# Thresholded attention and a quick-GELU MLP on one core: three of five threshold subtractions of the first eight head pairs on GpSimd, two-server transfers in the planner, new ranks

## The chip, the cores and the metric

The kernel runs on one core of a Trainium2 chip. The metric is device time in microseconds (us) of that core for one launch; lower is better. The time before the change is the median of three runs. One more execution was recorded by the profiler. Engines are named as the profile names them: PE (TensorE), DVE (VectorE), ACT (ScalarE), POOL (GpSimd), SP (SyncE, which here only issues transfers).

## The reference

Attention in fp32 with 8 batches, 8 heads, 576 rows and head size 64. Scores below the row maximum minus `tau` are dropped, the rest goes through a softmax. The result, laid out as 4608 tokens by 512, goes through an MLP with 2048 hidden units.

```python
scores = scale * np.matmul(q, k.transpose(0, 1, 3, 2))
thresh = np.max(scores, axis=-1, keepdims=True) - tau
scores = np.where(scores >= thresh, scores, -1000000000.0)
scores = scores - np.max(scores, axis=-1, keepdims=True)
attn = np.exp(scores)
attn = attn / (np.sum(attn, axis=-1, keepdims=True) + 1e-09)
x = np.matmul(attn, v)            # then (B,H,S,D) -> (B*S, H*D)
h = x @ w_in
g = h * (1.0 / (1.0 + np.exp(-1.702 * h)))
out = g @ w_out
```

The two weight matrices arrive as 64-bit floats, so the kernel turns them into fp32 itself.

## The kernel before, in words

**Attention.** Two heads make a pair; there are 32 pairs (`NP`), four to a batch, numbered from 0. A pair's transposed scores are cut into nine key blocks of 64, kept two by two in tiles of 128x1152 fp32: four full tiles and a tail tile of 128x576. For a pair the steps are, with their functions:

- `load_qk`, `load_v`: transfers issued by SP; `prep` (L477): two 32x32-block transposes on DVE.
- `scores_run` / `scores` (L493): matmuls on PE in 64x64 tiles; `keep` (L510): ACT copies each block from PSUM to SBUF.
- `in_groups` with max (L516): DVE transposes and reduces each tile; `over_tiles` (L525) and `over_halves` (L536, L542): DVE ends the row maxima and takes tau off.
- The row of thresholds is spread over all partitions: `turn_rows` (L553) on DVE, then `row_out` to DRAM and `row_in` back by SP. Pair 2 uses `spread_max` on DVE instead (`BY_DMA`).
- `sub` (L580): DVE subtracts the thresholds from each of the five tiles, in place. Both operands and the result are in SBUF.
- `mask` (L586) and `exps` (L590): ACT zeroes out what lies below and takes the exponential.
- `values` (L601) and, for pairs 0 to 4, `sums_by_pe` (L601): PE. From pair 5 on the softmax sums are made by DVE: `in_groups` with add, `over_tiles`, then either `one_group` (L643, L647) with `spread_sums` (L684, L686), used for pairs 5 to 7, or from pair 8 on `turn_sums` (L658 to L663) with the transfers `sums_out` and `sums_in` (`SUMS_BY_DMA`).
- `place_x` (L703): DVE multiplies by the reciprocal sums into the MLP's input tile.

**Weights.** 32 pieces of 128x512 numbers (16 of `w_in`, 16 of `w_out`). For each, `load_w` issues two transfers from POOL's queue (L428, L429); DVE and ACT make fp32 of it: `cv_ex` (L439, DVE), `cv_power` (L447, ACT), `cv_frac` (L453 and L457, DVE), `cv_end` (L465, DVE). `hold` (L484) is a small POOL copy that keeps the loads behind the preps of pairs 2 and 3.

**MLP.** 18 blocks of 256 tokens. The first two go together (`mm1_0` L758, `gelu_0` L764, `mm2` L740), and start when pairs 0 to 3 are placed and the first pieces of `w_in` are ready; blocks 2 to 13 use `mm1` (L718), `gelu` (L730) and a seven-product scheme for the second matrix (`product` L909, sums `s_sums` L875 to L877 and `s_last` L888 on POOL); the last four use it for both matrices.

**Order.** No engine's order is left to a compiler. Each piece of work is a `task` with an engine, a cost in us, a rank and what it needs; `run_in_order` plays the costs through and, whenever an engine is free in that play, gives it the ready task of lowest rank. The kernel is emitted in the order that results, so a rank or a cost changes only the order of instructions on each engine. At run time every engine works through its list in order and waits on semaphores. Ranks are the pair's number plus a bias by kind of task, in tables `EARLY` (pairs 0 to 3), `SECOND` (4 to 7), `LATER` (8 to 31), `CV` for conversions and `W_RANK`. MLP matmuls have the last rank, so PE takes them when no attention work is ready. A DMA is one SP task with a fixed `lag` until the data counts as there.

Of the kernel before, what the change touches and what calls it, by code (L numbers as in the profile page):

```python
# [19 lines left out]
P = 128  # L20
# [10 lines left out]
def kernel(  # L31
# [84 lines left out]
    stop = const.tile([P, 1], FP32, name="stop")  # L116
    shift = const.tile([P, 1], FP32, name="shift")
# [9 lines left out]
    for x in ("raw0", "raw1", "qkT0", "qkT1", "mb"):  # L127
# [6 lines left out]
        "exps": -11.47,  # L134
        "in_groups": 5.75,
        "keep": 10.66,
        "load_qk": -0.27,
        "load_v": 4.86,
        "mask": -2.66,
        "one_group": -15.86,  # L140
        "one_row": 12.67,
        "over_halves": -7.01,
        "over_tiles": -4.01,
        "place_x": -17.11,
        "prep": -11.73,
        "row_in": 20.49,
        "row_out": 4.47,
        "scores_run": 12.45,
        "spread_max": -1.73,
        "spread_sums": 7.14,  # L150
        "sub": 9.27,
        "sums_by_pe": 0.27,
        "sums_in": -9.39,
        "sums_out": 2.13,
        "turn_rows": -12.55,
        "turn_sums": -0.41,
        "values": 14.64,
        "w_sum": 4.11,
        "x_sum": -14.1,
    }  # L160
    SECOND = {
        "exps": -7.29,
        "in_groups": 20.95,
        "keep": 16.67,
        "load_qk": -8.88,
        "load_v": 5.53,
        "mask": 2.36,
        "one_group": 2.55,
        "one_row": -2.71,
        "over_halves": -12.07,  # L170
        "over_tiles": 2.86,
        "place_x": -20.26,
        "prep": 3.49,
        "row_in": -19.42,
        "row_out": -24.08,
        "scores_run": -7.99,
        "spread_max": -3.11,
        "spread_sums": -2.29,
        "sub": 14.98,
        "sums_by_pe": 35.93,  # L180
        "sums_in": 7.43,
        "sums_out": 4.05,
        "turn_rows": -3.84,
        "turn_sums": 4.03,
        "values": 11.79,
        "w_sum": -10.45,
        "x_sum": -10.98,
    }
    LATER = {
        "exps": 2.01,  # L190
        "in_groups": 10.37,
        "keep": -0.02,
        "load_qk": -6.6,
        "load_v": 3.77,
        "mask": 14.79,
        "one_group": 4.78,
        "one_row": -14.98,
        "over_halves": 1.09,
        "over_tiles": -6.27,
        "place_x": -0.34,  # L200
        "prep": 2.34,
        "row_in": 4.02,
        "row_out": 2.64,
        "scores_run": -11.25,
        "spread_max": -9.44,
        "spread_sums": -6.73,
        "sub": 2.14,
        "sums_by_pe": 1.46,
        "sums_in": 3.78,
        "sums_out": 2.16,  # L210
        "turn_rows": 12.26,
        "turn_sums": 0.29,
        "values": -10.38,
        "w_sum": 6.61,
        "x_sum": 6.02,
    }
    CV = {
        "cv_end": -8.05,
        "cv_ex": 2.22,
        "cv_frac": -11.72,  # L220
        "cv_power": -4.72,
        "load_w": -7.79,
    }

    LAG = {"PE": 0.26, "DVE": 0.18, "ACT": 0.22, "POOL": 0.18}

    QUARTERS = ("scores", "scores_run", "values", "sums_by_pe")
# [12 lines left out]
    FIRST, LAST = -9.0, 1000.0  # L240
    need, follows = {}, {}

    def run_in_order():
# [12 lines left out]
        while events:  # L256
# [18 lines left out]
            for engine, queue in ready.items():  # L275
                if engine in busy:
                    continue
                for rank, i in sorted(queue):
                    if engine == "PE" and held_for not in (None, i):
                        continue  # L280
                    take = tasks[i][6]
                    least = need.get(i, {})
                    if all(free[pool] >= take.count(pool) for pool in set(take)) and all(
                        free[pool] >= least[pool] for pool in least
                    ):
                        break
                else:
                    continue
                queue.remove((rank, i))
                for pool in take:  # L290
                    free[pool] -= 1
                busy.add(engine)
                cost = tasks[i][1]
                if engine == "PE":
                    held_for = follows.get(i)
                    last, mode = mode, tasks[i][3].__name__ in QUARTERS
                    cost += ENTER[mode] if mode != last else 0.0
                heapq.heappush(events, (now + cost, 0, i))
                started += 1
                tasks[i][3](*tasks[i][4])  # L300
# [3 lines left out]
    JOINT = 7  # L304

# [183 lines left out]
    def scores(n, j):  # L489
# [8 lines left out]
        if j == NK - 1:  # L498
            del mats[n, 0], mats[n, 1]
# [32 lines left out]
    def over_halves(n):  # L532
        r = stats[n, ALU.max]
        o = work.tile([P, QB], FP32, name="fold", tag="fold", bufs=1)
        for x in (1, 3) if n in BY_DMA else range(4):
# [3 lines left out]
            )  # L539
        if n in BY_DMA:  # L540
# [10 lines left out]
    def turn_rows(n):  # L551

        nc.vector.transpose(out=flat[1], in_=flat[0])  # L553

# [23 lines left out]
    def sub(n, t):  # L578
        s = sT[n, t].rearrange("p u h s -> p u (h s)")
        nc.vector.tensor_tensor(  # L580
            out=s, in0=s, in1=mbs[n].unsqueeze(1).to_broadcast(list(s.shape)), op=ALU.subtract
        )
# [24 lines left out]
    def values(n, tiles):  # L607
# [4 lines left out]
        if n < NPAIR:  # L612
# [334 lines left out]
    nc.gpsimd.memset(ones, 1.0)  # L947
    nc.gpsimd.dma_start(
# [26 lines left out]
    BY_PE = 5  # L975
    BY_DMA = (0, 1, *range(3, NP))
    SUMS_BY_DMA = range(8, NP)
    LEAD = 6
    WHOLE = 6

    FFU = 1.727
    T_RANK = FIRST

    W_RANK = (0, 12.87, 12.51, 22.24, 0, 4.97)
    ready_w, w_loads, w64 = [], [], 0
    for i in range(len(pieces)):
# [10 lines left out]
        a = task("POOL", 1.1, rank, load_w, i, after=w_loads[-1:], take=place, lag=9.0)  # L997
        w_loads.append(a)
        e = task("DVE", 0.345, rank, cv_ex, i, after=[a])
        m = task("ACT", 0.67, rank, cv_power, i, after=[e])  # L1000
        a = task("DVE", 1.1, rank, cv_frac, i, after=[e])

        over = [ready_w[y] for y in range(i) if i >= n_in and stage(y) == (i - n_in) // PER_STAGE]
        ready_w.append(task("DVE", 0.61, rank, cv_end, i, after=[a, m] + over, give=place))
# [191 lines left out]
    for n in range(NP):  # L1196
# [5 lines left out]
        slow = 1.1 if n < NPAIR else 1.0  # L1202
# [3 lines left out]
        cost = 3.5 if NPAIR <= n < 2 * NPAIR else 2.0  # L1206
        lag = (4.6, 3.0)[n] if n < 2 else 10.0 if n < 2 * NPAIR else 3.0
        lq = task("SP", cost, r - 2.0, load_qk, n, 0, q0, after=behind, take=own(n, "raw0"), lag=lag)
        lk = task(
            "SP", cost if n else 0.1, r - 2.0, load_qk, n, 1, q1, after=behind,  # L1210
            take=own(n, "raw1"), lag=lag,
        )
        v_m = f"v_m{n % 2}"
        lv = task("SP", 2.4, r + (1.85 if n < 2 else -1.2), load_v, n, after=lvs[-1:], take=(v_m,), lag=3.0)
        lvs.append(lv)
        pq = task("DVE", 0.69, r, prep, n, 0, after=[lq], take=own(n, "qkT0"), give=own(n, "raw0"))
# [45 lines left out]
        else:  # L1262
            for js in [range(x, x + 3) for x in range(0, NK, 3)] if n >= WHOLE else [[x] for x in range(NK)]:
# [4 lines left out]
                    give=own(n, "qkT0", "qkT1") if js[-1] == NK - 1 else (),  # L1268
# [4 lines left out]
        a = task("DVE", 0.35, r, over_tiles, n, ALU.max, after=mx)  # L1273
        a = task(
            "DVE", 0.8 if n in BY_DMA else 1.05, r, over_halves, n, after=[a, tau_done],
            take=("row",) if n in BY_DMA else (),
        )
        if n in BY_DMA:
            a = task("DVE", 0.21, r, turn_rows, n, after=[a])
            a = task("SP", 0.6, r, row_out, n, after=[a], lag=3.3)  # L1280
            m = task(
                "SP", 1.0, r, row_in, n, after=[a], take=own(n, "mb"), give=("row",),
                lag=5.2,
            )
        else:
            m = task("DVE", 0.78, r, spread_max, n, after=[a], take=own(n, "mb"))
        spread[n] = m
        ws, subs = [], [m]
        for t in range(NKT + 1):
            tail = t == NKT  # L1290
            a = task(
                "DVE", 0.67 if tail else 1.35, r, sub, n, t, after=subs[-1:],
                give=own(n, "mb") if tail else (),
            )
            subs.append(a)
# [5 lines left out]
        if n < NPAIR:  # L1301

            pv = den = None
            for t in every:
                first = t == 0
                den = task(
                    "PE", (0.97 if t < NKT else 0.484) * slow, r, sums_by_pe, n, [t], True, after=[ws[t], den],
                    take=("psM", "psM") if first else (),
                )
                pv = task(  # L1310
                    "PE", (0.97 if t < NKT else 0.484) * slow, r, values, n, [t], after=[ws[t], den, pv, lv],
                    take=("psA",) if first else (), give=(back[t],) if t < NKT else ("s_t", v_m),
                )
            su = []
            a = task("DVE", 1.07, r, one_row, n, after=[den], give=("psM", "psM"))
        else:
# [3 lines left out]
            if n < BY_PE:  # L1320
                a = task("PE", 4.36, r, sums_by_pe, n, every, False, after=ws + [pv], take=("psA",), give=back)
                a = task("DVE", 1.07, r, one_row, n, after=[a], give=("psA",))
            else:
                su = [
                    task("DVE", 0.66 if t == NKT else 1.27, r, in_groups, n, t, ALU.add, after=[ws[t]])
                    for t in range(NKT + 1)
                ]
                a = task("DVE", 0.35, r, over_tiles, n, ALU.add, after=su + [pv], give=back)
                if n in SUMS_BY_DMA:
                    a = task("DVE", 1.35, r, turn_sums, n, after=[a], take=("row_s",))  # L1330
                    a = task("SP", 0.6, r, sums_out, n, after=[a], lag=3.3)
                    summed[n] = task("SP", 1.0, r, sums_in, n, after=[a], take=("rc",), give=("row_s",), lag=5.2)
                else:
                    a = task("DVE", 1.6, r, one_group, n, after=[a])
# [41 lines left out]
```

## Time and profile before

| | us |
|---|---|
| median of three runs (1318.22 to 1318.92) | 1318.74 |
| the profiled execution, its own time | 1317.94 |
| its span, first to last instruction | 1316.2 |
| PE busy in the span | 1260.9 |
| DVE busy | 1006.1 |
| ACT busy | 646.6 |
| POOL busy | 249.0 |
| PE busy in 0 to 120 us | 79.00 |
| PE busy in 120 to 200 us | 79.05 |
| PE busy in 200 to 300 us | 94.19 |
| PE busy in 300 to 700 us | 397.42 |
| PE busy in 700 to 1100 us | 398.52 |
| PE busy in 1100 to 1316 us | 212.76 |

The profile is of one execution. A row of groups gives the line, the engine, the operation, what is written and read with shapes, how often, then busy time, mean duration in ns, and the idle time of the engine before these instructions with what ended it. The table's windows are read against their length: 120 us with 79.00 busy leave 41.0 idle. A clock below 1.00 is the share of full speed that TensorE was granted.

### The profile page before, as it was taken

How to read it: one execution, taken by the hardware profiler on the slowest of the kernel's cores; microseconds unless marked ns; L12 is line 12 of the kernel's file. 1: busy time of each engine (PE TensorE's matmuls, PEld its weight loads, DVE VectorE, ACT ScalarE, POOL GpSimd, SP SyncE). 2: the span in 40 equal slices, each digit the busy share in tenths (PEclk: the TensorE clock that was granted, in tenths of full speed). 3: DMA queues.
4: the chain of work that ended last, by engine and by line, in shares of the span. 5: the costliest groups of instructions: out<-in, count | busy, mean ns of one | idle time of the engine just before them, and what ended most of it. 6: DMA issues, size and time to landing. Idle time of an engine off the chain costs nothing. (4 is left out here: it accounts for less than half of the span.)

```text
span 1316.2 us, 22807 instructions
## 1 busy us (share of the span) xinstructions
PE 1260.9 (96%) x9128; PEld 975.6 (74%) x9128; DVE 1006.1 (76%) x1610; ACT 646.6 (49%) x830; POOL 249.0 (19%) x291
## 2 busy tenths in 40 slices
PE   5669999999999999999999999999999999999998
PEld 2346864457887777777778888777777778888887
DVE  7989999898888887788777877777888863652642
ACT  4876666576554555555554555454556540210210
POOL 1201211012031211213021303030212117120120
PEclk8879999999999999999999999999999999999999
DMA  8976766545323223212213222323122110000000
GB/s 152 293 189 207 230 207 149 112 77 100 85 55 71 55 55 71 51 50 54 58 42 72 55 71 55 71 55 71 36 55 54 36 46 8 9 1 25 8 0 32
DMA packets 258819, 102.88 MB, mean 78 GB/s; under 512 B 233754, under 2 KB 243994, under 8 KB 258714
## 3 DMA queue, kind: packets, MB, share of 16 engines
q1 hardware_dynamic: 244986, 63.40, 22.4%
q0 software_dynamic: 11360, 37.74, 9.3%
q8 instruction: 71, 1.16, 0.4%
q10 hardware_dynamic: 2368, 0.30, 0.2%
q14 instruction: 34, 0.28, 0.1%
HBM read 87.51 MB, written 9.69 MB: 74 GB/s over the span
## 5 line engine op out<-in xcount | busy, mean ns | idle before, releaser
L516 DVE TRANSPOSE_TENSOR_REDUCE part<-arena 128x36 f32<-128x1152 f32 (+1 forms) x295 | 357.5, 1235 | 41.9 <-ACT arena L510 32.4
L718 PE MATMUL hps<-xT,w_in 128*128 128x256 f32 x1536 | 337.2, 380 | 0.5 <-DVE arena L730 0.4
L718 PEld LDWEIGHTS hps<-xT,w_in 128*128 128x128 f32 x1536 | 290.7, 190 | 45.9 <-issue 5.7
L586 ACT ACTIVATE arena<-arena 128x1152 f32<-128x1152 f32 (+1 forms) x160 | 169.4, 1059 | 144.0 <-DVE arena L580 143.8
L510 ACT COPY arena<-ps 128x576 f32<-128x576 f32 x288 | 170.7, 647 | 115.3 <-PE ps L493 111.9
L580 DVE TENSOR_TENSOR arena<-arena 128x1152 f32<-128x1152 f32 (+1 forms) x158 | 201.1, 1313 | 20.5 <-DMA arena<-row 20.5
L909 PE MATMUL ops<-w_out,arena 128*128 128x256 f32 x896 | 202.4, 380 | 1.8 <-DVE arena L730 1.8
L590 ACT ACTIVATE arena<-arena,shift,scl 128x1152 f32<-128x1152 f32 (+1 forms) x160 | 200.3, 1252 | 4.1
L493 PE MATMUL ps<-arena 64*64 64x288 f32 x2304 | 174.7, 420 | 22.9 <-DVE arena L477 15.3
L909 PEld LDWEIGHTS ops<-w_out,arena 128*128 128x128 f32 x896 | 169.3, 190 | 28.7 <-DVE arena L730 3.1
L875 POOL TENSOR_TENSOR arena<-arena 128x256 f32<-128x256 f32 x56 | 49.7, 888 | 647.1 <-DVE arena L730 543.9
L601 PE MATMUL pv<-arena 64*64 64x288 f32 x2176 | 159.7, 408 | 0.0
L727 ACT ACTIVATE th<-hps 128x512 f32<-128x512 f32 x112 | 66.0, 589 | 186.0 <-PE hps L718 171.8
L909 PE MATMUL ops<-arena 128*128 128x256 f32 x672 | 150.7, 380 | 0.7 <-DVE osb L931 0.7
L493 PEld LDWEIGHTS ps<-arena 64*64 64x64 f32 x2304 | 84.0, 137 | 90.8 <-ACT arena L510 30.4
L909 PEld LDWEIGHTS ops<-arena 128*128 128x128 f32 x672 | 127.1, 190 | 20.4 <-issue 2.2
L601 PEld LDWEIGHTS pv<-arena 64*64 64x64 f32 x2176 | 82.1, 134 | 54.1 <-issue 10.0
L931 DVE SCALAR_TENSOR_TENSOR osb<-ops,osb 128x256 f32<-128x256 f32 x98 | 39.3, 413 | 97.9 <-PE ops L909 90.6
L730 DVE SCALAR_TENSOR_TENSOR arena<-th,hps 128x512 f32<-128x512 f32 x96 | 64.2, 669 | 46.7 <-ACT th L727 46.4
L740 PE MATMUL ops<-w_out,arena 128*128 128x512 f32 x128 | 57.2, 600 | 3.2 <-DVE w_out L465 2.2
L758 PE MATMUL hps<-xT,w_in 128*128 128x256 f32 x256 | 56.4, 381 | 0.0
L888 POOL TENSOR_TENSOR arena<-arena 128x512 f32<-128x512 f32 x28 | 35.6, 1272 | 108.3 <-PE ops L909 108.3
(115 smaller groups left out, 1044.7 us busy)
## 6 DMA issues: line engine op xcount, KB each, us to landing
arena<-in_v_dram SPq DMA_DIRECT2D x128, 144.0 KB
arena<-in_q_dram SPq DMA_DIRECT2D x128, 72.0 KB
out_dram<-osb SPq DMA_DIRECT2D x36, 256.0 KB
arena<-in_k_dram SPq DMA_DIRECT2D x124, 72.0 KB
arena<-row SPq DMA_DIRECT2D x62, 144.0 KB
arena<-row_s SPq DMA_DIRECT2D x48, 144.0 KB
w_out<-in_moe_w_in_dram POOLq DMA_DIRECT2D x12, 512.0 KB, 9.5
arena<-in_moe_w_out_dram POOLq DMA_DIRECT2D x12, 512.0 KB, 6.3
```

The costliest lines, as they stand in the source:

```text
L493: nc.tensor.matmul(ps[ts(c, KT), h, 0:SH], lhsT=mats[n, 1][ts(h, D), ts(j, KT)], rhs=mats[n, 0][ts(h, D), ts(c, SH)], start=True, stop=True,)
L510: nc.scalar.copy(out=sT[n, t][:, u], in_=pss.pop((n, j))[:, :, 0:SH])
L516: nc.vector.tensor_reduce(out=stats[n, op][:, t * 2 * QB : min(2 * t + 2, NK) * QB], in_=sT[n, t].rearrange("p u h (g d) -> p (u h g) d", ...
L580: nc.vector.tensor_tensor(out=s, in0=s, in1=mbs[n].unsqueeze(1).to_broadcast(list(s.shape)), op=ALU.subtract)
L586: nc.scalar.activation(out=s, in_=s, func=AF.Prelu, alpha=STEEP)
L590: nc.scalar.activation(out=s, in_=s, func=AF.Exp, scale=scl, bias=shift)
L601: nc.tensor.matmul(o[c][ts(h, D), 0:SH], lhsT=left(j, h)[ts(c, KT)], rhs=sT[n, t][ts(c, KT), u, h, :], start=(j == 0), stop=(j == NK - 1),)
L718: nc.tensor.matmul(hidden[j][:, ts(f, BLK)], lhsT=w_in[:, c, ds((f * HF + j) * P, P)], rhs=xTs[blk][:, c, :], start=(c == 0), stop=(c == N ...
L727: nc.scalar.activation(out=ths[j], in_=hidden[j], func=AF.Tanh, scale=GELU_SCALE / 2)
L730: nc.vector.scalar_tensor_tensor(out=g[:, :, j, :], in0=two(ths.pop(j)), scalar=1.0, in1=two(hidden.pop(j)), op0=ALU.add, op1=ALU.mult,)
L740: nc.tensor.matmul(acc[i], lhsT=g0[:, j, ts(i, P)], rhs=w_out[:, j, :], start=(j == 0), stop=(j == NFC - 1),)
L909: nc.tensor.matmul(banks[blk][k][:, ts(o, HM)], lhsT=left[:, j, :], rhs=right[:, j, :], start=(j == 0), stop=(j == HF - 1),)
```

## The change

- Subtraction: `sub` runs on GpSimd for tiles 1, 3 and 4 (the tail) of pairs 0 to 7, and stays on VectorE for tiles 0 and 2. Its waits within a pair are per engine.
- Sums: pairs 5, 6 and 7 go by `turn_sums` and two transfers each way, as pairs from 8 on did.
- Planner: a transfer is now a task of its own on one of two servers, "DMS" for what SP issues and "DMW" for the weights, taken first come first served; SP tasks keep only their issue cost. Costs of conversions and some others are new; `cv_frac` and `cv_end` are charged `SHARED` = 0.2 us more.
- Ranks: all four tables and `W_RANK` are new.
- A second way to apply thresholds by PE (`row_blocks`, `again`, `mask_one`) is added but its set of pairs, `TWICE`, is empty. Its two constant tiles are still filled at the start, on POOL ahead of the transfer of tau.

```diff
+    minus = const.tile([P, 2, KT], FP32, name="minus")
+    own_row = const.tile([P, QB // 2], FP32, name="own_row")
...
     EARLY = {
...
-        "in_groups": 5.75,
+        "in_groups": 13.97,
...
-        "sub": 9.27,
+        "sub": 6.54,
...
     CV = {
-        "cv_end": -8.05,
-        "cv_ex": 2.22,
-        "cv_frac": -11.72,
-        "cv_power": -4.72,
-        "load_w": -7.79,
+        "cv_end": -15.81,
+        "cv_ex": -1.62,
+        "cv_frac": -18.99,
+        "cv_power": -9.27,
+        "load_w": -20.76,
     }
...
+    def transfer(by, time, a, give=(), lag=1.7):
+        return task(by, time, FIRST, moved, after=[a], give=give, lag=lag)
...
+    TWICE = ()
+    BY_POOL = dict.fromkeys(range(8), (1, 3, 4))
...
     def sub(n, t):
         s = sT[n, t].rearrange("p u h s -> p u (h s)")
-        nc.vector.tensor_tensor(
+        engine = nc.gpsimd if t in BY_POOL.get(n, ()) else nc.vector
+        engine.tensor_tensor(
             out=s, in0=s, in1=mbs[n].unsqueeze(1).to_broadcast(list(s.shape)), op=ALU.subtract
         )
...
+    nc.gpsimd.memset(minus, 0.0)
+    nc.gpsimd.memset(own_row, 0.0)
+    for x in range(4):
+        nc.gpsimd.memset(minus[ts(x, 32), x % 2, :], -1.0)
+        nc.gpsimd.affine_select(
+            out=own_row[ts(x, 32)], in_=own_row[ts(x, 32)], compare_op=ALU.not_equal, fill=1.0,
+            base=-(QB // 2) * (x // 2), pattern=[[-1, QB // 2]], channel_multiplier=1,
+        )
...
-    SUMS_BY_DMA = range(8, NP)
+    SUMS_BY_DMA = range(5, NP)
...
+    SHARED = 0.2 if BY_POOL else 0.0
...
-    W_RANK = (0, 12.87, 12.51, 22.24, 0, 4.97)
+    W_RANK = (22.52, 3.88, 13.03, 23.19, 4.19, 0.55)
...
-        a = task("DVE", 1.1, rank, cv_frac, i, after=[e])
+        a = task("DVE", 1.14 + SHARED, rank, cv_frac, i, after=[e])
...
-        ready_w.append(task("DVE", 0.61, rank, cv_end, i, after=[a, m] + over, give=place))
+        ready_w.append(task("DVE", 0.7 + SHARED, rank, cv_end, i, after=[a, m] + over, give=place))
...
-        ws, subs = [], [m]
+        spread.setdefault(n, m)
+        ws, subs = [], [(m, None)]
...
+            pool = t in BY_POOL.get(n, ())
             a = task(
-                "DVE", 0.67 if tail else 1.35, r, sub, n, t, after=subs[-1:],
+                "POOL" if pool else "DVE", (1.45 if pool else 0.67) if tail else 2.7 if pool else 1.35,
+                r, sub, n, t, after=[y for y, x in subs if tail or x in (None, pool)],
                 give=own(n, "mb") if tail else (),
             )
-            subs.append(a)
+            subs.append((a, pool))
```

## The prediction, as put on record

> **What bounds the kernel now.** I read the page's busy table first, then busy time by stages.
>
> ```profile
> PE 1260.9 (96%) x9128; PEld 975.6 (74%) x9128; DVE 1006.1 (76%) x1610; ACT 646.6 (49%) x830; POOL 249.0 (19%) x291
> ```
>
> PE is busy in 1260.9 of 1316.2 us, so 55.3 us are all that any reordering can win. The windows say where they lie (columns: length, PE, weight loads, DVE, ACT, POOL, PE clock, DMA share, GB/s).
>
> ```profile
> 0.00:120.00 120.00, 79.00 (x1016) 45.33 (x1016) 103.53 (x179) 87.16 (x110) 18.74 (x43) 0.87 0.81 208
> 120.00:200.00 80.00, 79.05 (x494) 59.24 (x490) 77.93 (x135) 45.16 (x58) 15.93 (x29) 1.00 0.67 214
> 200.00:300.00 100.00, 94.19 (x727) 49.38 (x727) 92.04 (x142) 68.01 (x86) 10.11 (x11) 0.98 0.57 116
> ```
>
> 41.0 of the 55.3 us are idle before 120 us, 6.8 between 120 and 300, 7.5 in the remaining thousand. DVE is busy in 103.5 of the first 120 us (it can't start before 6.8) and in 77.9 of the next 80. PE's waits in 0 to 120 us name their releasers:
>
> ```profile
> PE ps L493 <- DVE arena L477: 15.3, 3, 8.3
> PE den L601 <- DVE r L632: 12.9, 2, 10.8
> PE den L601 <- DVE w_out L457: 7.0, 1, 7.0
> PE den L601 <- ACT arena L590: 2.8, 6, 1.1
> ```
>
> The first three add up to 35.2 of 41.0 us. So up to about 240 us DVE's list sets the pace; afterwards PE does. The MLP's first matmul starts at 117.6 us. A microsecond taken off DVE's list ahead of that brings the rest of PE's work forward by about one, as long as DVE also keeps up from 120 to 240, where it is as full.
>
> **What the Trainium skill says.** "GPSIMD Engine Reference", section 3.1 Elementwise — side-by-side cycle accounting, puts a two-input operation on GpSimd at about 2.6 cycles of 1.2 GHz per element, roughly twice VectorE. The trace agrees: POOL's undisturbed two-input operations took 0.73 us at 256 elements and 1.27 at 512, so 2.11 ns an element. "SBUF — State Buffer", section Who interferes with whom, says that GpSimd shares one pair of SBUF ports with VectorE, exclusively for a whole instruction, and that a VectorE instruction with two SBUF inputs is held by a GpSimd one that reads SBUF. The trace shows it, in DVE's and POOL's order of time (start, duration):
>
> ```profile
> 1088.52 0.69 DVE L797 TENSOR_TENSOR arena<-w_in 128x512 f32<-128x512 f32 x1
> ...
> 1092.53 1.75 DVE L806 TENSOR_TENSOR xT<-xT 128x512 f32<-128x512 f32 x1
> ```
> ```profile
> 1092.02 1.71 POOL L797 TENSOR_TENSOR arena<-w_in 128x512 f32<-128x512 f32 x1
> ```
>
> 0.69 us is the undisturbed length of that shape. POOL's instruction waited some 0.44 us (1.71 for 1.27), then ran to 1093.73; DVE's, begun at 1092.53, took 1.06 us too long. "VectorE: DVE Perf Modes", section Mode 2×_2P — use both read ports for one tensor, says that one-source fp32 operations from SBUF may take both ports too. The two L536 instructions at 291.2 us took 1.14 instead of 0.49 beside POOL, which agrees; a conversion beside a POOL operation isn't in this trace.
>
> **The change part by part.** I sum against the profiled execution's 1317.94 us (span 1316.2 and 1.7 around it); the median of the runs is 0.8 above it. Durations, from DVE's groups up to 280 us:
>
> ```profile
> L580 DVE TENSOR_TENSOR arena<-arena 128x1152 f32<-128x1152 f32 x36 | 47.0, 1342 | 7.5 <-DMA arena<-row 7.5
> L457 DVE SCALAR_TENSOR_TENSOR w_out<-w_out 128x512 int32<-128x512 int32 x16 | 11.1, 695 | 0.5
> L439 DVE TENSOR_SCALAR arena<-arena 128x512 uint32<-128x512 uint32 x16 | 6.8, 426 | 0.0
> L580 DVE TENSOR_TENSOR arena<-arena 128x576 f32<-128x576 f32 x7 | 5.2, 749 | 0.0
> ```
>
> *Subtractions off DVE.* 8 pairs x (2 x 1.342 + 0.749) = 27.5 us, half before 117.6 us.
>
> *Sums of pairs 5 to 7.* `one_group` with `spread_sums` took 0.73 + 0.70 + 0.27 + 0.78 = 2.48 us on DVE; `turn_sums` of pair 8 took 0.71 + 0.18 + 0.27 + 0.21 = 1.37. Three times the difference is 3.3 us. Six transfers out and six in are added. For pair 8 SP began them at 289.48, DVE placed its result at 299.61: the way by DRAM is some 8 us longer in latency than DVE's own 1.05. Pair 7 is placed at 276.40 and block 2 starts on PE at 280.23. Its sum can begin before its values do (261.6), so I take nothing; without that lead up to 4 us. Gross saving: 30.8 us.
>
> *Subtractions on POOL.* 1.27 + 640 x 2.11 ns = 2.62 us for a full tile and 1.41 for the tail: 16 x 2.62 + 8 x 1.41 = 53.2 us. As POOL idled most of the first 240 us, its own time is hidden. Three of them take 6.65 us against the 6.12 of five on DVE before, so ACT, which needs all five, gets its last tile at about the same time. Behind a POOL subtraction that waits for its row stand `hold`, `load_w` and their two transfers a piece. POOL waited 36.3 us for a free stage at one point, so I take nothing; if its refills get late, up to 4 us.
>
> *Collisions.* This is the unknown. While POOL holds the ports, DVE goes on through `in_groups` (L516), preps and what reads PSUM, and stops at the first instruction with two SBUF inputs or two ports: the remaining subtractions, conversions, `over_halves`. Nearest rows: 32 conversions x (0.42 + 0.42 + 0.70 + 0.69) = 71.4 us, remaining subtractions 16 x 1.342 = 21.5, `over_halves` about 8; 101 us of some 190 after the removal, about half. Upper bound: every hold stops DVE for its whole length, 53.2 us. Lower bound: the change's own charge, 0.2 on two tasks of 32 pieces, 12.8 us. A gain is excluded, as a lock only delays. If half of the holds met such an instruction at once, it would be 27; as a burst of L516 (1.35 us each) hides part, I take 22.
>
> *Start.* Ten small POOL instructions now stand before the transfer of tau. Fills of 128x32 and 128x64 took 0.12 and 0.15 us, so some 1.5 us in all; tau's transfer was issued at 1.39, took 3.9, and DVE read it at 9.16. There is 3.1 us of cover: 0. An `affine_select` isn't in the trace; if it is ten times a fill, 4 us of start are lost.
>
> *Ranks and servers.* They remove no instruction. What they could win is DVE's own idle time after its start, 12.5 us from 10 to 240, its longest waits 3.7 for a row behind loads on SP (SP issued q and k of a later pair ahead of `row_out` at 82.19). What they could lose is as much, since the new order was laid out with subtractions on DVE at 1.35, that is without collisions. Value 0, from -5 to +8. `LATER` acts where PE idles 7.5 us in 1016; at most a few of these either way.
>
> *Sum.* 30.8 - 22 = 8.8 us less DVE work up to 240 us. ACT (87.2 us of the first 120) and DMA (share 0.81) are late next, but have that much room. 1317.94 - 8.8 = 1309.1; with the 0.8 to the median, 1310.
>
> **Rivals.** *Slower: DVE behind POOL's locks.* POOL's tile 1 and DVE's tile 0 are released by the same row. Whoever comes second waits, and then DVE's tile 2 finds POOL in tile 1: 2.4 us a pair. If in the two holds that follow (tile 3 and tail, 4.0 us) conversions stand next, 60% of them are lost as well: 4.8 a pair, 38.5 in all. Then DVE has 7.7 us more to go through, and the time is 1317.94 + 7.7 + 0.8 = 1326. For it: subtractions and conversions were back to back from 34.7 to 64 us, and the new `CV` ranks put conversions ahead of both `in_groups` and `sub`. Against: `in_groups` is the largest group and passes. It decides from 30.8 us of collisions on, 58% of POOL's hold time.
>
> *The saving is parked.* PE's start may be set by ACT, the loads (DMA share over 1.00 in three of the first eight slices of 10 us) or the row trips, and DVE only gets idle: 1318.7, within 0.2%. Against: DVE's waits for a row were only 3.9 us up to 240.
>
> *Collisions at their lower bound.* 30.8 - 12.8 = 18.0 saved: 1317.94 - 18.0 + 0.8 = 1301. For it: PE idles 41 us, enough to be won. Against: the alternation near 1090 us.
>
> **Numbers.** Forecast 0.40 at 1310, its own range 1305 to 1315; collisions at the lower bound 0.11 at 1301; parked 0.11; slower 0.38 at 1326. About 0.2% (2.6 us) is what a measurement of this kernel can tell from no change. Faster 0.51, same 0.11, slower 0.38. The range reaches from 1299, a little past the small-collision case, to 1331, the slower rival with the late tau or the refills on top; beyond each lies about one in ten.
>
> **What would show it.** Right: POOL has 24 more two-input instructions of 2.6 and 1.4 us or longer, DVE's busy sum to 300 us changes little, since waits for the port count as duration, L457, L465 and L580 get longer means, and the MLP's first matmul comes some 5 us before 117.6. Means of L580 above 2.0 us or of L457 and L465 above 1.0 would show the slower rival; PE waiting for a row or for L510 the parked one. What would make it wrong in another way: stalls after 300 us from the new `LATER` ranks, or block 2 waiting for pair 7.

## The result and the profile after

The changed kernel took 1352.17 us in the median of four runs (1350.22 to 1353.76), the kernel before 1318.83 beside it: ratio 1.0247, 95% interval 1.0224 to 1.027. The forecast was 1310 and the end of its range 1331. The loss of 33.3 us is more than four times the 7.3 us that the slower rival had (1326 against 1318.7). The profiled execution took 1350.22 us, with a span of 1348.4.

The busy table of the page after:

```profile
PE 1267.5 (94%) x9128; PEld 984.7 (73%) x9128; DVE 1014.9 (75%) x1577; ACT 638.1 (47%) x830; POOL 312.5 (23%) x325
```

DVE has 33 instructions fewer and is busy 8.8 us longer; POOL is busy 63.5 us longer. PE has the same matmuls and 6.6 us more busy time (its granted clock in the first 120 us is 0.80 instead of 0.87). Its idle time went from 55.3 to 1348.4 - 1267.5 = 80.9 us. The stages, in the same columns as before:

```profile
0.00:120.00 120.00, 64.33 (x801) 38.92 (x805) 100.45 (x134) 74.36 (x94) 52.41 (x63) 0.80 0.75 191
120.00:200.00 80.00, 73.61 (x586) 58.46 (x579) 70.18 (x120) 37.89 (x50) 18.78 (x25) 0.93 0.62 180
200.00:300.00 100.00, 87.69 (x564) 45.41 (x566) 83.10 (x123) 61.73 (x78) 34.47 (x23) 0.95 0.57 134
```

PE idles 55.7 us before 120, 6.4 up to 200 and 12.3 up to 300: 74.4 against 47.8, so all the idle time that was added lies ahead of 300 us. In the first 120 us DVE is as busy as before (100.45 against 103.53) and gets through 134 instructions instead of 179; 12 of the 45 that are missing are subtractions that went to POOL. The MLP's first matmul comes at 134.8 us instead of 117.6. DVE's groups up to 300 us answer to those shown of before (L633 is the old L580, L469 the old L457, L451 the old L439, L477 the old L465; the number after the busy time: mean ns):

```profile
L633 DVE TENSOR_TENSOR arena<-arena 128x1152 f32<-128x1152 f32 x16 | 40.2, 2537 | 10.9 <-DMA arena<-row 10.9
L477 DVE SCALAR_TENSOR_TENSOR w_in<-w_out 128x512 f32<-128x512 int32 x12 | 14.3, 1192 | 5.8 <-ACT w_out L459 5.7
L469 DVE SCALAR_TENSOR_TENSOR w_out<-w_out 128x512 int32<-128x512 int32 x16 | 14.3, 894 | 0.6
L548 DVE TENSOR_SCALAR fold<-red,gap 32x18 f32<-32x18 f32 x20 | 9.8, 492 | 0.6
L451 DVE TENSOR_SCALAR w_out<-w_out 128x512 uint32<-128x512 uint32 x16 | 9.4, 586 | 0.0
```

The 16 full-tile subtractions left on DVE take 40.2 us, where 36 took 47.0 before (the lines of before are in the prediction). From here on **held time** means this: for every shape of DVE instruction up to 320 us, the time by which its durations exceed the median of that shape in the kernel before, added up. It is 1.2 us in the kernel before and 38.8 after: 16 x (2.537 - 1.342) = 19.1 in subtractions, 7.6 in `cv_end`, 3.2 in `cv_frac`, 5.2 in `over_halves`, 3.8 in `cv_ex`. The forecast had 22, the slower rival 38.5.

How such a hold reaches PE is seen at 151 us. DVE's order of time (start, duration), then PE's:

```profile
151.22 9.36 DVE L633 TENSOR_TENSOR arena<-arena 128x1152 f32<-128x1152 f32 x2
160.50 1.36 DVE L528 TRANSPOSE_TENSOR_REDUCE part<-arena 128x36 f32<-128x1152 f32 x1
161.80 0.64 DVE L817 SCALAR_TENSOR_TENSOR arena<-th,hps 128x512 f32<-128x512 f32 x1
```
```profile
162.50 12.73 PE L811 MATMUL hps<-xT,w_in 128*128 128x256 f32 x44 [5.70 <-DVE arena L817]
```

Two subtractions worth 2.7 us take 9.36. The first layer's gelu (L817) stands behind them in DVE's list, PE needs the PSUM bank that it frees, and PE stands still for 5.70 us.

### The profile page after: what moved, and what is told of

Same layout as the page of the kernel before. It is cut to its first block, busy times and chain, and to the rows that moved or that the text cites. A ratio compares the mean times of both kernels' runs of the same rounds, so it can differ in the third digit from the quotient of the medians.

```text
span 1348.4 us, 22852 instructions
## 1 busy us (share of the span) xinstructions
PE 1267.5 (94%) x9128; PEld 984.7 (73%) x9128; DVE 1014.9 (75%) x1577; ACT 638.1 (47%) x830; POOL 312.5 (23%) x325
## 4 chain that ended last, share of the span: by engine, by line
PE 73%; DVE 12%; DMA 6%; ACT 5%; issue 3%; POOL 1%; SPq 1%; DVEq 0%; POOLq 0%; ACTq 0%
PE ops L962 23%; PE hps L771 22%; PE pv L654 8%; PE ps L505 7%; PE ps L876 4%; PE ps L962 4%; DMA arena<-row 3%; PE ops L876 3%; DVE part L528 3%; DVE arena L633 3%; DMA row<-flat 2%; ACT arena L522 1%; ACT arena L643 1%; ACT arena L639 1%; PE hps L811 1%
## 5 line engine op out<-in xcount | busy, mean ns | idle before, releaser
L771 PE MATMUL hps<-xT,w_in 128*128 128x256 f32 x1536 | 337.4, 380 | 0.9 <-DVE arena L783 0.8
L771 PEld LDWEIGHTS hps<-xT,w_in 128*128 128x128 f32 x1536 | 290.5, 190 | 46.8 <-issue 5.3
L639 ACT ACTIVATE arena<-arena 128x1152 f32<-128x1152 f32 (+1 forms) x160 | 165.8, 1060 | 160.9 <-DVE arena L633 141.2
L505 PE MATMUL ps<-arena 64*64 64x288 f32 x2304 | 177.5, 421 | 39.8 <-DVE arena L489 16.3
L633 DVE TENSOR_TENSOR arena<-arena 128x1152 f32<-128x1152 f32 (+1 forms) x136 | 194.2, 1470 | 26.2 <-DMA arena<-row 25.9
L643 ACT ACTIVATE arena<-arena,shift,scl 128x1152 f32<-128x1152 f32 (+1 forms) x160 | 194.9, 1249 | 1.4
L505 PEld LDWEIGHTS ps<-arena 64*64 64x64 f32 x2304 | 87.1, 137 | 104.2 <-ACT arena L522 38.6
L962 PEld LDWEIGHTS ops<-arena 128*128 128x128 f32 x672 | 127.3, 190 | 19.3 <-issue 2.2
L984 DVE SCALAR_TENSOR_TENSOR osb<-ops,osb 128x256 f32<-128x256 f32 x98 | 39.3, 413 | 91.9 <-PE ops L962 85.7
L633 POOL TENSOR_TENSOR arena<-arena 128x1152 f32<-128x1152 f32 (+1 forms) x22 | 60.9, 2808 | 47.2 <-DMA arena<-row 33.8
L811 PE MATMUL hps<-xT,w_in 128*128 128x256 f32 x256 | 61.1, 400 | 6.7 <-DVE arena L817 6.7
L811 PEld LDWEIGHTS hps<-xT,w_in 128*128 128x128 f32 x256 | 50.8, 201 | 17.6 <-DVE arena L817 8.4
```

The source lines that it names most:

```text
L505: nc.tensor.matmul(ps[ts(c, KT), h, 0:SH], lhsT=mats[n, 1][ts(h, D), ts(j, KT)], rhs=mats[n, 0][ts(h, D), ts(c, SH)], start=True, stop=True,)
L633: engine.tensor_tensor(out=s, in0=s, in1=mbs[n].unsqueeze(1).to_broadcast(list(s.shape)), op=ALU.subtract)
L639: nc.scalar.activation(out=s, in_=s, func=AF.Prelu, alpha=STEEP)
L643: nc.scalar.activation(out=s, in_=s, func=AF.Exp, scale=scl, bias=shift)
L771: nc.tensor.matmul(hidden[j][:, ts(f, BLK)], lhsT=w_in[:, c, ds((f * HF + j) * P, P)], rhs=xTs[blk][:, c, :], start=(c == 0), stop=(c == N ...
L811: nc.tensor.matmul(hidden[j][:, ts(i, BLK)], lhsT=w_in[:, c, ts(j, P)], rhs=xTs[i][:, c, :], start=(c == 0), stop=(c == NDC - 1),)
```

## The experiments

Times are medians. Ratios are to the kernel before, run beside each, with their 95% intervals; they aren't quotients of the medians, so the two can differ by a few us.

**Order and locks apart.** "Lock" is short for this: a DVE instruction that has begun is held while one of POOL's runs. The first kernel keeps the order of instructions of the changed kernel and puts every subtraction back on DVE. The second keeps the old order and changes nothing but the engine.

```diff
 # same_order_dve, from the changed kernel
-        engine = nc.gpsimd if t in BY_POOL.get(n, ()) else nc.vector
-        engine.tensor_tensor(
+        nc.vector.tensor_tensor(
 # before_order_pool, from the kernel before
-        nc.vector.tensor_tensor(
+        engine = nc.gpsimd if n < 8 and t in (1, 3, 4) else nc.vector
+        engine.tensor_tensor(
```

> The changed kernel with every list of instructions in its new order, but all threshold subtractions issued on DVE at the places that the planner gave them. Theory of the locks (DVE held behind GpSimd's subtractions is the cause): DVE gets 27.5 us of work back but loses about 38 us of waiting, and what was late behind it comes earlier; at most 1338 us, and the means of the held DVE instructions are back at 1.34 and 0.69 us. Theory of the order (new ranks and servers are the cause): DVE has more to do in the same order, 1346 us or more.

> The kernel before with its order of instructions untouched on every engine, except that the three subtractions of pairs 0 to 7 are taken out of DVE's list and put in GpSimd's at the same place. Theory of the locks: the 27.5 us saved are more than eaten up by held DVE instructions, 1325 to 1350 us, with L580 on DVE at a mean above 2.0 us. Theory that the move is good and only the new order is bad: 1300 to 1314 us.

1332.86 us, ratio 1.010 (1.0064 to 1.0136), and 1332.43, ratio 1.011 (1.0076 to 1.0145). Both lie where the theory of the locks had them. GpSimd's part is 1352.17 - 1332.86 = 19.3 us in the new order and some 14.5 in the old. The new order costs 13 us by the ratio and 16 by the medians with nothing on GpSimd (1332.86 against 1317.02 beside it). It was laid out for subtractions on GpSimd, so part of this may be that mismatch; an order laid out for DVE alone (replanned_dve, below) is no better. Held time is 0.7 us in the first and 30.4 in the second. In the old order DVE's own work thus changed by 30.4 - 27.5 = +2.9 us and the time by 14.5. A sum of DVE's microseconds doesn't give the time. It also matters who waits for the held instructions: ACT's waits for `sub` up to 300 us grew by 18.9 us from the kernel before to this one:

```profile
ACT arena L586 <- DVE arena L580: 27.4, 13, 5.3
```
```profile
ACT arena L587 <- DVE arena L581: 42.7, 12, 8.6
ACT arena L587 <- POOL arena L581: 3.6, 4, 2.4
```

**Locks alone.** Here every subtraction stays on DVE in the old order, and GpSimd gets 40 instructions with two SBUF inputs that nobody waits for.

```diff
 # pool_dummies, from the kernel before, in sub for n < 8 and t in (1, 3, 4)
+            x = mbs[n][:, 0:512]
+            for _ in range(s.shape[1]):
+                nc.gpsimd.tensor_tensor(out=idle, in0=x, in1=x, op=ALU.subtract)
```

> The kernel before in its own order, with all subtractions on DVE as they were; beside them GpSimd runs, at the places where the moved subtractions stood, operations of 512 elements with two SBUF inputs (the thresholds twice, into a tile that nobody reads): two for each of tiles 1 and 3, one for tile 4, 40 in all, about 51 us. No engine ever waits for a result of them. Theory of the locks: DVE is held for 25 to 45 us although nobody needs GpSimd, 1330 to 1355 us. Theory of the slow subtraction (the moved tiles come late because GpSimd takes 2.6 us, and ACT waits for them): nothing waits, 1316 to 1321 us.

1334.71 us, ratio 1.0119 (1.0101 to 1.0137). Held time is 20.0 us, less than the 25 to 45 expected, and the time rises by 15.7. This kernel does all the work of the old one, and nobody waits for a result of the added instructions. The weight loads stand behind them in POOL's list, but up to 300 us neither DVE nor ACT has a wait for one in this trace. So the lock alone makes a kernel slower. It doesn't say that the lock is all there is in the changed kernel, where ACT also waits for POOL's own tiles (below). Its groups up to 300 us:

```profile
L584 POOL TENSOR_TENSOR idle<-arena 128x512 f32<-128x512 f32 x40 | 62.9, 1572 | 29.5 <-DMA arena<-row 26.3 <-DVE arena L558 0.8
L585 DVE TENSOR_TENSOR arena<-arena 128x1152 f32<-128x1152 f32 x36 | 57.5, 1633 | 5.0 <-DMA arena<-row 5.0
```

**Where DVE does something else meanwhile.** In the old order pairs 2 and 7 alone have reductions between their subtractions in DVE's list; the others have conversions, gelus, preps or nothing there. One kernel moves only these two pairs, another only the tails of eight pairs.

```diff
+        engine = nc.gpsimd if n in (2, 7) and t in (1, 3, 4) else nc.vector   # pool_pairs_2_7
+        engine = nc.gpsimd if n < 8 and t == 4 else nc.vector                 # pool_tails
```

> The kernel before in its own order, with the three subtractions on GpSimd for pairs 2 and 7 only. In the run with all eight pairs DVE was held 0.1 and 0.4 us in these two, since its list has reductions between the subtractions there. Theory of the locks: 6.9 us of DVE work saved, half of it where DVE sets the pace, under 2 us of holds: 1312 to 1318 us. Theory of the slow subtraction: a quarter of the loss of all eight pairs, 1320 to 1323 us.

> The kernel before in its own order, with only the tail tile's subtraction of pairs 0 to 7 on GpSimd. It waits for nothing but the thresholds and so runs beside DVE's first subtractions. Theory of the locks: 6.0 us of DVE work saved against eight holds of at most 1.4 us, mostly in full, since a subtraction stands next on DVE: 1317 to 1325 us. Theory of the slow subtraction: the tail is ready before it is needed, so only the saving stays, 1312 to 1316 us.

The pairs: 1316.70 us (14 runs, 1314.49 to 1326.08), ratio 0.9991 (0.9975 to 1.0008), no difference that can be told. The tails: 1322.86, ratio 1.0026 (1.0014 to 1.0039). The pairs took 2 x 3.43 = 6.9 us off DVE and were held for 1.7; the tails took 6.0 off and were held for 6.5. DVE and POOL in pair 2:

```profile
70.78 1.49 DVE L581 TENSOR_TENSOR arena<-arena 128x1152 f32<-128x1152 f32 x1
72.20 2.62 DVE L516 TRANSPOSE_TENSOR_REDUCE part<-arena 128x36 f32<-128x1152 f32 x2
...
77.87 1.32 DVE L581 TENSOR_TENSOR arena<-arena 128x1152 f32<-128x1152 f32 x1
```
```profile
68.42 7.71 POOL L581 TENSOR_TENSOR arena<-arena 128x1152 f32<-128x1152 f32 x3 [0.89 <-DVE arena L557]
```

The reductions run at their full speed beside POOL: 1.31 us each, where the mean in the kernel before was 1.35. The Trainium skill ("SBUF — State Buffer", section Who interferes with whom) says as much of DVE instructions with one SBUF input outside the two-port modes, and this trace agrees. So what stands in DVE's list can keep held time near that of the kernel before. Still, 5.2 us net off DVE brought some 1.2 us, by the interval between a gain of 3.3 and a loss of 1.1.

**What a new plan costs.** Each of these lets the planner lay the order out again after one part of the change, with all subtractions on DVE except in the third. The last two are controls that change nothing but a cost which the planner assumes.

```diff
-    BY_POOL = dict.fromkeys(range(8), (1, 3, 4))
+    BY_POOL = {}                                    # replanned_dve, from the changed kernel
...
 # before_new_planner: old ranks and sums, no filled constants, the rest of the new planner
 # before_pool_subs: old planner and ranks; tasks of sub on POOL at 2.7 and 1.45 us
 # before_new_ranks: the old kernel with the new tables and W_RANK
-    SUMS_BY_DMA = range(8, NP)
+    SUMS_BY_DMA = range(5, NP)                      # before_sums_rows
-        e = task("DVE", 0.345, rank, cv_ex, i, after=[a])
+        e = task("DVE", 0.36, rank, cv_ex, i, after=[a])     # before_cv_ex
...
 # before_conv_costs: cv_ex 0.42, cv_frac 1.14, cv_end 0.70, as the trace has them
```

> The changed kernel with BY_POOL empty, so that the planner lays out a new order with its new ranks, subtractions on DVE and no 0.2 us charge. Theory of the locks: near the kernel before, 1312 to 1326 us. Theory of the order: 1338 us or more, since ranks and servers stay.

> The changed kernel with the old ranks, subtractions on DVE, sums by rows from pair 8 on and without the unused constants: what is left of the change is the planner, its two servers and its costs. If the servers and costs make the bad order: 1330 us or more. If the new ranks make it: 1315 to 1324 us.

> The kernel before with only the three subtractions of pairs 0 to 7 moved to GpSimd (its ranks, its lags, planner costs 2.7 and 1.45 us for GpSimd). Theory of the locks: the same collisions as in the changed kernel, 30 to 40 us of held DVE time, 1335 to 1360 us. Theory of the order: 1308 to 1328 us, as the old order has less waiting.

> The kernel before with only the new rank tables, under the old planner. If the new ranks make the bad order: 1328 us or more. If the servers and costs make it: 1315 to 1324 us. Both this run and the planner's alone above 1328 would say that ranks and planner only fit as a pair, and that either change of one spoils the old order.

> The kernel before with only the sums of pairs 5 to 7 by rows. Both theories: DVE has 3.3 us less to do between 190 and 270 us, where PE hardly waits for it: 1315 to 1321 us. Over 1322 us would mean that the longer way of the sums holds up the placing of a pair.

> A second, smaller control: the kernel before with one cost of the planner changed, cv_ex 0.36 us instead of 0.345. No instruction changes, but the order does. If any new order loses what the old ranks were fitted to: 1325 to 1350 us. If the first control lost because of its particular costs: 1314 to 1322 us.

> A control: the kernel before with the planner's costs of cv_ex, cv_frac and cv_end set to what the trace shows (0.42, 1.14, 0.70 us instead of 0.345, 1.1, 0.61). No instruction changes, only the order. If a new order costs little in itself: 1314 to 1322 us. If any new order loses what the old ranks were fitted to: 1325 to 1345 us.

| kernel | us | ratio (95%) |
|---|---|---|
| replanned_dve | 1344.61 | 1.0199 (1.0170 to 1.0227) |
| before_new_planner | 1343.67 | 1.0192 (1.0163 to 1.0220) |
| before_pool_subs | 1359.40 | 1.0305 (1.0273 to 1.0337) |
| before_new_ranks | 1343.44 | 1.0186 (1.0154 to 1.0218) |
| before_sums_rows | 1330.52 | 1.0089 (1.0061 to 1.0116) |
| before_cv_ex | 1326.40 | 1.0060 (1.0042 to 1.0078) |
| before_conv_costs | 1346.45 | 1.0214 (1.0183 to 1.0246) |

The two controls say most. An assumed cost that is moved by 0.015 us gives an order that is 8 us slower; costs corrected to what the trace shows give one that is 28 us slower. All six new plans without subtractions on GpSimd lose 8 to 28 us, the new ranks alone and the new planner alone among them. So a run with a new plan says little about the part that was changed in it: the 11.7 us of before_sums_rows can't be put down to rows against DVE (its trace is level with the old one up to some 190 us and then has PE stalls of 6.3 us at 270 and 7.4 at 316). Only kernels with one order can be set side by side.

**Where in the new order.** In the trace of same_order_dve (an execution of 1337.15 us, the slowest of its four), DVE waits 17.8 us for threshold rows between 10 and 240 us; in the kernel before 3.9. The three long waits, of pairs 1, 3 and 5:

```profile
53.45 1.36 DVE L632 TENSOR_TENSOR arena<-arena 128x1152 f32<-128x1152 f32 x1 [5.63 <-DMA arena<-row]
...
102.42 2.63 DVE L632 TENSOR_TENSOR arena<-arena 128x1152 f32<-128x1152 f32 x2 [5.87 <-DMA arena<-row]
...
194.12 1.36 DVE L632 TENSOR_TENSOR arena<-arena 128x1152 f32<-128x1152 f32 x1 [6.31 <-DMA arena<-row]
```

Pair 1's row leaves at 40.00 us here, at 28.77 before. Three kernels move only the four tasks that make and send that row, without a new plan:

```diff
 # four tasks of pair 1: over_halves, turn_rows, row_out, row_in
 # same_order_early_row, after_early_row: to just behind over_tiles(1) and row_in(0)
 # before_late_row: the old order, to just behind sub(0, 0), the first of pair 0's five
+        for f, a in emitted[:at] + row + emitted[at:]:
+            f(*a)
```

> The changed kernel's order with all subtractions on VectorE (1332.9), but the four steps of pair 1's threshold row (its last maximum, its turn, row out, row in) moved forward to just behind its over_tiles and pair 0's row_in. If the late row of pair 1 makes the order's loss: 1328 or less, since the wait of 5.63 us for that row at 53 us goes and PE's first MLP matmul comes up to 5 us before 132.5. If the loss is spread over many places: 1331 or more.

> The kernel before with one thing of the new order: the same four steps of pair 1's row moved back, to just behind pair 0's subtractions, so that the row goes out about 10 us later. If a late row of pair 1 makes the order's loss: 1323 to 1330. If the loss is spread over many places, or the list absorbs the delay: 1317 to 1321.

> The changed kernel with pair 1's row moved forward as in the first of these three. It also takes the two small instructions of over_halves out of the stretch in which GpSimd held them for 5.75 us. If the late row of pair 1 makes the order's loss: 1345 or less from 1352. If the loss is spread over many places: 1349 or more.

1328.37 us, ratio 1.0074 (1.0055 to 1.0094); 1322.56, ratio 1.0034 (1.0019 to 1.0048); 1351.46, ratio 1.0252 (1.0231 to 1.0273). Back in the old order the late row costs 4.6 us, with an interval clear of no change; DVE then waits 4.86 us for it. Forward in the new order it gives 4.5 us by the medians and 3.4 by the ratios, whose intervals overlap, so this gain is likely but not shown. Both fall just short of what was asked (1323 and 1328). In the changed kernel the early row brings nothing. DVE's wait for that row was only 0.36 us there, and the trace of after_early_row shows where the held time went: `over_halves`, which had been held at 37 us, now comes earlier, and the conversions that stand next are held in its place.

```profile
37.54 5.86 DVE L477 SCALAR_TENSOR_TENSOR w_out<-w_out 128x512 int32<-128x512 int32 x1
...
47.86 8.28 DVE L459 TENSOR_SCALAR w_out<-w_out 128x512 uint32<-128x512 uint32 x1
```

They are worth 0.69 and 0.42 us. Held time stays what it was, within 0.5 us.

The next kernel puts ready work in front of the other two long waits. Two more ask the same of the one such wait in the kernel before (3.70 us at 88.56), the second of them with pairs 2 and 7 on POOL as above.

```diff
 # same_order_filled, on top of same_order_early_row
+            (("sub", 3, 1), [("cv_end", 8), ("cv_ex", 9), ("cv_frac", 9), ("cv_ex", 10), ("cv_frac", 10)]),
+            (("sub", 5, 1), [("cv_end", 23), ("gelu_0", 11), ("cv_ex", 24), ("cv_frac", 24)]),
 # before_filled and filled_pool_2_7, from the kernel before
+        first, ahead = ("sub", 3, 0), [(x, i) for i in (7, 8, 9) for x in ("cv_ex", "cv_frac")]
```

> The new order with all subtractions on VectorE and pair 1's row early (1328.4), and besides that 6.6 us of ready VectorE work moved in front of the two subtractions that still wait longest for their row: conversions worth 2.9 us and more ahead of pair 3's (waits 6.67 us at 98 us), conversions and the first-layer gelu that PE waits for ahead of pair 5's (waits 5.88 us at 184 us). If VectorE's waits for rows are what the new order costs: 1320 to 1325, about 4 to 7 us less, and PE's wait of some 5 us on that gelu goes. If not: 1327 or more.

> The kernel before with the first halves of conversions 7, 8 and 9 (3.3 us of VectorE) moved in front of pair 3's subtractions, which wait 3.70 us for their row at 88.56. If VectorE's waits for rows before the MLP's start are paid in full: 1315 to 1317. If they are absorbed, or the moved work only delays pair 3: 1318 to 1321.

> The same with three of five subtractions of pairs 2 and 7 alone on GpSimd, the two pairs in which VectorE has reductions between its own subtractions. If both parts are worth what they are alone: a microsecond or two under the run with the moved conversions alone, 1313 to 1316. If conversions now stand beside GpSimd's subtractions and are held: 1318 or more.

1327.91 us (five runs, 1323.28 to 1333.14), ratio 1.0075 (1.0048 to 1.0101); 1318.45, ratio 0.9994 (0.9983 to 1.0005); 1314.78, ratio 0.9981 (0.9965 to 0.9997). The first misses what was asked: the median hasn't moved. Yet in its trace DVE's row waits between 10 and 240 us fell from 15.7 to 5.9 us and PE's waits for the first layer's gelu up to 300 us from 6.5 to 1.2, and the profiled execution took 1323.51. The executions scatter more than those of most other kernels, and why they do stays open. With rows waited for 5.9 us, little more than the 3.9 of the kernel before, the median is still 9 us above it: by this run the waits for rows are not the main part of what the new order costs. The second kernel shows one place where such a gain goes. DVE's waits between 10 and 240 us, before and with the moved conversions:

```profile
DVE arena L580 <- DMA arena<-row: 3.9, 2, 3.7
DVE w_in L465 <- ACT w_out L447: 1.3, 2, 0.8
```
```profile
DVE w_in L474 <- ACT w_out L456: 4.7, 3, 3.8
```

The wait for the row is gone, and DVE waits 3.4 us longer for ACT's part of the same conversions, which had stayed in its place. The MLP starts 0.8 us earlier; the time is the same. The third kernel is the only one whose interval lies below the kernel before, by 0.2%. It only just excludes no change, it is one of many comparisons, and its 14 runs fall into two groups (8 from 1313.3 to 1314.9 and 6 from 1319.6 to 1322.1), so a gain isn't shown.

## Why the prediction was wrong

**The two steps that failed.** "As a burst of L516 hides part, I take 22": held time was 38.8 us, 73% of POOL's 53.2, and not 41%. The share of DVE's list that can be held is not the share of holds that meet it: the remaining subtractions are released by the same row as POOL's and were held in six of the eight pairs, and conversions queued right beside POOL's in pairs 0 to 3 and 5. And "Value 0, from -5 to +8" for ranks and servers: the new order costs 13 to 16 us with nothing on GpSimd. The prediction named DVE's wait for rows as what could be won. It grew instead, from 3.9 to 17.8 us, and this explains only a part of the loss (see Open).

**The sum.** With the two measured terms it reads 1318.7 - 30.8 + 38.8 + 15 = 1342 and is still 10 us short. So its rule, "a microsecond taken off DVE's list" for "about one" at the end, fails as well. For kernels whose order is the same, in us:

| kernel | off DVE | held | net | time |
|---|---|---|---|---|
| pool_pairs_2_7 | 6.9 | 1.7 | -5.2 | -1.2 |
| pool_tails | 6.0 | 6.5 | +0.5 | +3.4 |
| before_order_pool | 27.5 | 30.4 | +2.9 | +14.5 |
| pool_dummies | 0 | 20.0 | +20.0 | +15.7 |
| after, against same_order_dve | 27.5 | 38.1 | +10.6 | +19.3 |

(Time is the ratio less one, times 1318, and in the last row the difference of medians. Held contains the 1.2 us of the kernel before, except in the last row.) The net misses the time by 3 to 12 us. Two factors fit all five within about 1 us: 0.8 us lost for a microsecond held, 0.37 won for one taken off. For the changed kernel that is 0.8 x 38.1 - 0.37 x 27.5 = 20.3 for 19.3 measured, for before_order_pool 24.3 - 10.2 = 14.1 for 14.5. The factors are fitted to these runs, and the times are themselves uncertain by 2 to 5 us. A sixth pair of one order that was not used for the fit, after_early_row against same_order_early_row, gives 20.5 for 23.1 measured (held 38.4, off 27.5). So they are rough. By them held time has to stay under about half of the time taken off for a gain, where the prediction had 100% of it: 30.8. Why a microsecond taken off brings so little is not shown. It may not have been the last to be waited for, or the moved tiles come later from POOL and ACT waits for them.

**The subtractions on POOL.** Their durations were right: 2.61 to 2.64 us and 1.39 to 1.42 undisturbed, for 2.62 and 1.41. But DVE delays POOL too, and the 24 took 65.7 us and not 53.2. "ACT gets its last tile at about the same time" was wrong. Pair 1's five tiles should have taken 6.65 us; from 53.63 to 63.03 they took 9.4. POOL's and DVE's order of time:

```profile
53.67 6.88 POOL L633 TENSOR_TENSOR arena<-arena 128x1152 f32<-128x1152 f32 x2 [3.97 <-DMA arena<-row]
60.52 2.51 POOL L633 TENSOR_TENSOR arena<-arena,arena 128x576 f32<-128x576 f32 x1
```
```profile
53.63 1.36 DVE L633 TENSOR_TENSOR arena<-arena 128x1152 f32<-128x1152 f32 x1 [0.36 <-DMA arena<-row]
54.91 3.14 DVE L477 SCALAR_TENSOR_TENSOR w_in<-w_out 128x512 f32<-128x512 int32 x1
57.97 3.80 DVE L633 TENSOR_TENSOR arena<-arena 128x1152 f32<-128x1152 f32 x1
```

Each engine waits for the other in turn: this is the slower rival's picture, tile by tile, with a conversion held in between. Its mechanism was right. That its 38.5 us came so close is partly luck: the 2.4 us that it gave to the subtraction of every pair were lost in pairs 1, 2, 3, 6 and 7, nothing in 0 and 5, and 6.75 in pair 4. Its 1326 left out the order. ACT's waits for `sub` after, up to 300 us, add up to 39.3, against 27.4 before and 25.3 in same_order_dve:

```profile
ACT arena L639 <- DVE arena L633: 19.7, 7, 6.4
ACT arena L639 <- POOL arena L633: 19.6, 7, 7.4
```

DVE in turn waited 12.4 us for ACT's part of the conversions between 10 and 240 us, against 1.3 before and 3.5 in same_order_dve. How much of the 19.3 us goes this way and how much straight from held DVE instructions to PE is not measured.

**What held.** The start cost nothing: tau's transfer was issued at 2.85 us instead of 1.39, and DVE read it at 7.84 instead of 9.16. POOL's refills came in time: between 10 and 240 us DVE has no wait for a weight load. "Means of L580 above 2.0 us or of L457 and L465 above 1.0" was to show the slower rival: 2.54 did for the full tiles. L465 passed 1.0 only in the group shown (1.19; 0.93 over all 32 conversions), and L457 did not (0.79 over all). What was said of DVE's busy sum to 300 us, little change, was wrong: it fell from 273.5 to 253.7, as DVE stood idle for longer; over the span it rose by 8.8. After 300 us PE idles 6.5 us, against 7.5 before, so the new `LATER` ranks cost nothing there. The sums by rows aren't measured alone, since no kernel here has them in the old order.

**Open.** Of the 13 to 16 us of the new order, the late row of pair 1 accounts for 3 to 5: shown when it is moved back in the old order, likely when it is moved forward in the new one. Two more waits for rows were filled, and the median did not shift. What makes up the rest, some 9 us, is open. That an order which is fitted to its costs breaks in many small places agrees with the controls, but is argued, not shown.

## What to carry to other kernels

An instruction with two SBUF inputs that moves to GpSimd can hold DVE for longer than it took there (38.1 and 30.4 us held here for 27.5 taken off), unless DVE has one-input reductions to do meanwhile: look at what stands next in DVE's list, not at shares of it. Where a fitted plan orders the work, first change the engine or the cost alone in the unchanged order, and run a control that only jolts the planner, before a result is put down to a part of the change. A wait that is filled with ready work has gained nothing until it is seen who is late next.

## What the runs showed of the hardware

A waiting DVE instruction isn't always served next. POOL's and DVE's subtractions at 152 us in the changed kernel (count; shortest, median and longest in ns; first and last start):

```profile
L633 POOL TENSOR_TENSOR arena<-arena x3: 1391/2614/2642, 152.8 to 158.0; 128x1152 f32<-128x1152 f32 x2, 128x576 f32<-128x576 f32 x1
L633 DVE TENSOR_TENSOR arena<-arena x2: 1352/4724/8095, 151.2 to 152.5; 128x1152 f32<-128x1152 f32 x2
```

DVE's second began at 152.5 us and took 8.1 instead of 1.35: three of POOL's passed it in a row, undisturbed. The Trainium skill ("SBUF — State Buffer", section Who interferes with whom) has whoever issues first take the shared ports for its whole instruction; here DVE's began 0.3 us before POOL's first and came after all three. POOL was issuing a transfer at that moment, as it was when the conversion at 47.86 us of after_early_row began, which came after four of POOL's. But in before_order_pool at 182.77 us no transfer was being issued, and a DVE subtraction that had begun 1.6 us after POOL's first came after POOL's second too (4.83 us). So a transfer alone doesn't explain it, and why the two took turns at 53 us stays open as well. A tiny instruction was held as long as a large one. Two L548 of 32x18 numbers, worth 0.23 us each, took 5.75 beside two subtractions on POOL:

```profile
37.24 5.75 DVE L548 TENSOR_SCALAR fold<-red,gap 32x18 f32<-32x18 f32 x2
```
```profile
37.49 5.19 POOL L633 TENSOR_TENSOR arena<-arena 128x1152 f32<-128x1152 f32 x2
```

Integer conversions with one source are held too: one L451 took 1.79 us instead of 0.42 at 48.20, beside POOL's tail, and the one in after_early_row took 8.28.
